# Splitting the first loads of an adaLN / windowed-attention / token-mixer kernel between two DMA queues, with a new instruction order

## The chip, the cores and the metric

The kernel runs on one core of a Trainium2 chip. The metric is the device time of one execution in microseconds. Times before: 201.69, 201.56 and 201.41 us, median 201.56.

A core has five instruction streams that run beside each other and meet through semaphores: TensorE (PE: matmuls, with weight loads as PEld), VectorE (DVE), ScalarE (ACT), GpSimd (POOL) and SyncE (SP). SyncE issues DMAs and nothing else; ScalarE can issue DMAs too, on a queue of its own that is part of its instruction stream.

## What is computed

```python
def reference(A_x, A_wqkv, A_wo, B_x, B_w1, B_b1, B_w2, B_b2, c, w_mod):
    mod = (silu(c) @ w_mod).reshape(1, 6, 1, 512)
    sa, ca, ga, sb, cb, gb = mod[:, 0], mod[:, 1], ..., mod[:, 5]
    h = layernorm(x) * (1 + ca) + sa
    x = x + ga * A(h, A_wqkv, A_wo)
    h = layernorm(x) * (1 + cb) + sb
    return x + gb * B(h, B_w1, B_b1, B_w2, B_b2)
```

`x` is 2048 tokens by 512 channels, bf16. `A` is attention with 32 heads of 16 channels, in which each token sees 8 earlier tokens at a distance of 0, 2, ..., 14. `B` normalises each token, then mixes over the tokens for each channel: 2048 to 1792 with a tanh GELU, and back to 2048.

## The kernel before

The tokens lie in 16 tiles of 128. Attention goes through them in five chunks of 2, 4, 4, 4 and 2 tiles (`SIZES`). For each chunk the kernel takes layer norm statistics per tile (`ln1s`, `ln1v`), the group's reciprocal deviation (`rstd1_`, two ScalarE activations) and its offset (`nb1_`, VectorE), normalises each tile (`n1_`), transposes (`tr` and `hT` through TensorE for chunks 0 and 1, `xt` by DMA for the others), projects to q, k and v (`qkv<chunk>_<t><j>`, t = 0 query, 1 key, 2 value), evicts (`ev`), multiplies q and k on VectorE (`qk`), sums by matmul (`red`), does the softmax (`max`, `sub`, `exp`, `esum`, `rcp`, `smB`), multiplies with v on VectorE (`pv`), sums (`pvacc`), evicts (`oev`) and multiplies with the output weights (`wo`). A residual sum and two more layer norms follow (`x1`, `ln2`, `n2`, `aff`, `ln3`, `h3`), then the token mixer in two passes (`mlp1`, `mlp2`) and the stores.

At the start the condition `c` is loaded (`ld_c`), put through a SiLU (`cps`, `silu_exp`, `silu_dve`) and multiplied with the modulation weights: `ld_wmod1` loads the columns of the scale `ca`, `modcols1` and `a1col` make the column of 1 + ca from them, with which the weights or the transposed tiles are scaled (`wsc`, `hT`); `ld_wmod0`, `modcols0` and `sab` do so for the shift `sa`, and `qvb` makes the projections' bias of it. `ld_x0` and `ld_x1` load one tile each (chunk 0), `ld_x_<chunk>_<tile>` two tiles (256 KB); `ld_wqkv0`, `ld_wqkv1`, `ld_wqkv2` load the query, key and value weights, 512 KB each, as are `ld_wmod1` and `ld_wmod0`.

Every piece of work is added to a graph with the engines that could do it (`add_any`). Which engine does it and in which order the streams are issued is written by hand in the string `ORDER` (lines 191 to 249): a name takes the first engine of its list, and a letter behind a colon picks another (`a` ScalarE, `d` VectorE, `p` GpSimd, `s` SyncE; `q` on a matmul issues it as four column quarters). `schedule` (line 86) walks the string; each engine gets its own pieces in that order and works through them strictly in it. `fill:n` puts n units of 128 columns of matmuls with the identity matrix on TensorE, whose results nobody reads.

`dma` (line 376) issues on SyncE's queue; `dma2` (line 381) can issue on SyncE's or ScalarE's. The program that is built from this gives every DMA one of eight semaphores in turn, and a DMA that takes a semaphore for a second time waits, on the queue that issues it, until the earlier one has landed.

In the order before, ScalarE's queue holds `ld_x_1_2` and `ld_c`, then the load of the activation table, then its activations. SyncE's holds `ld_x1`, `ld_x0`, `ld_x_1_4`, `ld_wmod1`, `ld_x_2_8`, `ld_wqkv0`, `ld_x_2_6`, `ld_wqkv1`, `ld_wmod0` and the later loads.

Instructions are recorded through a wrapper, so that nearly all of them carry line 142 in the profile; they are told apart by tiles: `xx` the tokens, `big` (`wmodA`) the modulation columns and later the products, `wst` the raw projection weights, `h` the normalised tiles, `psS` and `psL` accumulators.

Of the kernel before, what the change touches and what calls it, by code (L numbers as in the profile page):

```python
# [196 lines left out]
qkv0_00 qvb0 wsc0_0:p ev0_10:a ld_b2 ld_wo1 hT1_1:d qkv1_00 ln1s11:d ln1s10:d ln1s13:d qkv1_10:q ln1v11 ln1v10
qvb_cp0:a ev0_00:a ln1s12:a ev0_02:d qkv1_13 ld_wqkv2 qkv0_20 ln1v13 qk0_3 qk0_2 ev1_13:a qk0_0 qvb1 ln1v12 qkv0_22:q
ld_wrow0 red0_0 ev1_00:a qkv1_03:q ev1_10:a qk0_1 red0_1 red0_2 red0_3 mask qvb_cp1:a ev0_20:a ev0_22:a wsc1_2:p
halo_v1:a qk1_0 ev1_03:a wsc1_3:a qkv1_11:q ld_wmod2 wsc2_3:a modrow0 ld_b1 mrows0:a ev1_11:a ld_wrow2 qkv1_02 max0  # L200
wsc0_2:p ld_wo0 n1_7:p sub0 rstd1_3 qkv1_01 ld_wo2 exp0 qkv1_12:q wsc1_1:p esum0:q qk1_3 red1_0 ev1_01:a qk1_1
ev1_02:a biascols n1_6:p ld_wrow1 rcp0 smB0 ev1_12:a ld_x_4_14 ln1s14:a qkv1_22 qk1_2 a2_0_2:a xt6 ld_wrow3 modrow1
red1_1 a2_0_1:a n1_9:p wsc2_0:d ln1s15:a ln1v14 nb1_3 n1_11:a qkv1_23:q mrows1 qkv1_21 ev1_21:a red1_2 red1_3 xt8
ev1_23:a fill:1 n1_10:p qkv1_20 ev1_20:a ev1_22:a qkv2_13 qkv2_10 wsc0_1:p vd0_2 ev2_13:a ln1v15 vd0_1 max1 sub1
qkv2_00 exp1 a2_0_0:s a2_0_3:s pv0_1 vd0_0 pv0_0 st_row0 pv0_2 qkv2_03 esum1:q ld_wo3 pvacc0_0 vd0_3 halo_v2:p
biascols_cp:a pvacc0_1 pv0_3 pvacc0_2 pvacc0_3 ev2_10:a ev2_00:a qk2_0 n1_13:a n1_12:a ld_row0 woq_s rcp1 smB1
oev0_2:a qkv2_11 qkv2_02:q ev2_03:a qk2_3 qkv2_01:q red2_0 oev0_0:a wo0:q wsc2_1:a wsc2_2:a qkv2_12 ev2_11:a ev2_01:a
ev2_02:a ev2_12:a wo1 qkv2_21:q a2_1_1:a qkv2_22 x1_1:a ln2q1:a x1_0:a xt10 ln2q0:a qk2_1 qkv2_23 xt12 qk2_2 a2_1_0:s
halo_k3:a ln2m0 vd1_2 a2_1_2:s qkv3_12 a2_1_3:s pv1_2 rstd1_4 red2_1 nb1_4 vd1_0 st_row1 red2_2 red2_3 rstd2_0
ev2_22:a nb2_0 ev2_21:a qkv3_13:q ev3_13:a max2 vd1_3 pv1_0 n1_14:a vd1_1 pvacc1_2 n1_15:a qkv2_20:q ev2_20:a sub2  # L210
qkv3_22:q ev3_12:a pv1_1 qkv3_10 exp2 ev2_23:a halo_v3:a qkv3_20 n2_0:a oev1_2:a ev3_10:a esum2 rcp2 qkv3_00 ev3_22:a
qkv3_02:q ev3_00:a pv1_3 ev3_02:a pvacc1_0 ev3_20:a qkv3_01:q ev3_01:a qkv3_11:q xt14 ld_row1 n2_1:p vd2_3 pvacc1_1
smB2 aff0 qk3_0 vd2_1 fill:1 vd2_0 oev1_0:a oev1_1:a pvacc1_3 ev3_11:a qk3_1 qkv3_23:q oev1_3:a a2_2_2:s ln3s1:a
qkv3_03:q wo4 a2_2_1:s qk3_2 a2_2_0:s ev3_03:a ev3_23:a x1_4:a ln2q4:a wo2 x1_2:a a2_2_3:s red3_0 wo3:q x1_3:a ln2q3:a
qkv3_21:q ev3_21:a wo5 red3_1 pv2_3 x1_5:a vd2_2 qk3_3 qkv4_20:q red3_2 qkv4_22 red3_3 qkv4_12 fill:18 ln2q5:a
ld_w1_0_512 ln2q2:a ln2m2 pv2_0 pvacc2_0 vd3_0 ev4_20:a ln3s0:a ln3v0 ev4_12:a rstd2_2 ev4_22:a ln3v1 qkv4_02 oev2_0:a
ln2m4 rstd2_4 nb2_2 n2_2:a max3 sub3:q exp3 pvacc2_3 oev2_3:a qkv4_10:q pv2_2 vd3_2 esum3 nb2_4 pv2_1 vd3_1 n2_3:p
ld_w1_0_0 n2_5:a rcp3 smB3 pvacc2_2 fill:14 a2_3_0:s a2_3_1:s a2_3_3:s n2_4:a qkv4_00:q oev2_2:a rstd3_0 aff2 pvacc2_1
oev2_1:a wo6 wo9 wo7 aff4 nb3_0 ln3s2:d ev4_02:a ln3s3:a ln3v3 h3_1:p wo8 a2_3_2:s ev4_00:a ln3v2 ld_w2_0 ln3s4:d
rstd3_2 nb3_2 x1_9:a ln3s5:a h3_0:p mlp1_0_6_0:q x1_7:a ln3v4 x1_8:a h3_3:d mlp1_0_1_0 h3_2:d mlp1_0_6_2 mlp1_0_1_2  # L220
pv3_1 mlp1_0_5_0:q ln3v5 ev4_10:a ld_w1_0_896 x1_6:a mlp1_0_3_0:q mlp1_0_3_2:q ln2q7:a pvacc3_1 rstd3_4 mlp1_0_5_2:q
oev3_1:a mlp1_0_2_0:q pv3_0 mlp1_0_2_2:q nb3_4 h3_4:a mlp1_0_0_0:q mlp1_0_0_2 h3_5:a mlp1_0_0_4:q qk4_0 ln2q8:a
ln2q6:a park0_0:a ln2q9:a mlp1_0_6_4:q mlp1_0_2_4:q mlp1_0_1_4:q park0_1:a pv3_2 mlp1_0_5_4:q vd3_3 pvacc3_0 oev3_0:a
mlp1_0_3_4:q ld_w2_1 park0_2:a pv3_3 red4_0 ln2m6 pvacc3_2 oev3_2:a mlp1_0_4_0:q qk4_1 pvacc3_3 ld_w1_0_1152
mlp1_0_4_2:q mlp1_0_4_4:q rstd2_6 oev3_3:a wo12:q halo_v4:p vd4_2 vd4_3 nb2_6 n2_9:a qk4_2 n2_7:d qk4_3 wo10:qn red4_1
ld_w1_0_1408 n2_6:a vd4_1 n2_8:a aff6 red4_2 red4_3 max4 park0_3:a ln3s8:d ln3s6:d x1_12:a ln3v8 wo11 vd4_0 ln3s9:d
mlp1_0_7_0 ld_w2_3 park0_4:a ln3v6 mlp1_0_7_2 park0_5:a ln3v9 x1_11:a ln2q12:a mlp1_0_8_0 mlp1_0_8_2 park0_6:a wo13:n
ln3s7:a ln3v7 sub4 mlp1_0_10_0 mlp1_0_9_0 x1_13:d exp4 rstd3_6 nb3_6 esum4 mlp1_0_8_4 ln2q13:a ln2m12 mlp1_0_10_2
mlp1_0_10_4 mlp1_0_9_2 rcp4 mlp1_0_7_4 h3_8:d rstd2_12 mlp1_0_12_0 mlp1_0_12_2 mlp1_0_12_4 smB4 a2_4_1:a a2_4_0:s
mlp1_0_9_4 a2_4_2:s h3_9:d a2_4_3:a h3_7:d nb2_12 h3_6:p mlp1_0_7_6 ln2q11:a park0_7:a x1_10:d mlp1_0_8_6 ld_w1_0_1664  # L230
ln2q10:a park0_8:a n2_13:p mlp1_0_9_6 park0_9:a n2_12:d aff12 ln2m10 rstd2_10 mlp1_0_10_6 park0_10:a ln3s13:a pv4_2
nb2_10 ld_w1_1_0 pv4_1 mlp1_0_11_0 mlp1_0_11_2 mlp1_0_11_4 mlp1_0_12_6 pv4_0 mlp1_0_11_6 ld_w1_1_640 inj1_6:qn pv4_3
pvacc4_0 pvacc4_1 n2_11:a mlp1_0_13_0:q pvacc4_2 pvacc4_3 n2_10:a mlp1_0_13_2:q park0_11:a mlp1_0_13_4 oev4_0:a
oev4_2:a aff10 ln3s10:a wo14 inj1_3:n ln3s11:d ln3v11 x1_14 ln2s14 wo15 x1_15 mlp1_0_13_6 ln2v14 ln3s12:a ln3v10
ln2s15 rstd2_14 nb2_14 ln2v15 n2_14:d rstd3_10 aff14 rstd2_15 nb2_15 inj1_4:qn ln3v13 park0_12:a mlp1_1_3_6 park0_13:a
mlp1_1_6_6 inj1_1:n mlp1_1_1_6 n2_15:p mlp1_1_4_6 inj1_0:n mlp1_1_0_6 nb3_10 h3_10:a mlp1_1_4_10 mlp1_1_3_10 ln3s14:d
ld_w2_4 mlp1_1_0_10 ln3v14 ln3v12 rstd3_12 h3_11:a mlp1_1_6_10 inj1_5:n mlp1_1_5_6 mlp1_1_5_10 rstd3_14 mlp1_1_1_10
aff15 nb3_12 ln3s15:d ln3v15 h3_12:p nb3_14 park1_0:+ h3_13:p rstd3_15 nb3_15 inj1_2:n mlp1_1_2_6 ld_w1_1_896 h3_14:p
h3_15:a ld_w1_2_0 park1_1:+ mlp1_1_2_10 park1_2:+ mlp1_1_7_10 park1_3:+ park1_4:+ park1_5:+ mlp1_1_8_10 mlp1_1_10_10
park1_6:+ padd1_7 padd1_10 gelu10 padd1_8 mlp1_1_9_10 padd1_9 gelu9 mlp1_2_4_11 mlp1_2_4_14 mlp1_2_1_11 mlp1_2_1_14  # L240
padd2_1 padd2_4 gelu7 mlp1_2_0_11 mlp1_2_0_14 padd2_0 gelu0 mlp1_2_2_11 gelu4 gelu8 mlp1_2_2_14 ld_w1_1_1408
mlp1_2_3_11 mlp1_2_3_14 padd2_3 gelu3 ld_w1_2_640 mlp1_2_6_11 padd2_6 gelu6 padd2_2 gelu2 mlp1_2_5_11 mlp1_1_11_10
padd1_11 mlp1_2_5_14 padd2_5 gelu1 gelu11 mlp1_1_12_10 ld_w2_5 ld_w2_7 mlp1_1_13_10 gelu5 mlp2_0_0 padd1_12 gelu12
mlp2_0_0b ld_w2_2 ld_w2_9 ld_w2_13 ld_w2_11 padd1_13 gelu13 mlp2_0_0c mlp2_6_0 mlp2_4_0 gsc fin0_0 st_out0_0 fin4_0
st_out4_0 mlp2_8_0 fin8_0 mlp2_3_0 fin3_0 mlp2_2_0 fin2_0 st_out2_0 mlp2_1_0 fin1_0 mlp2_7_0 st_out3_0 fin6_0
st_out6_0 fin7_0 mlp2_10_0 fin10_0 st_out7_0 mlp2_11_0 mlp2_5_0 st_out1_0 fin5_0 st_out5_0 mlp2_14_0 fin11_0
# [829 lines left out]
```

## Time and profile before

| | |
|---|---|
| median of three runs | 201.56 us |
| the profiled execution | 202.11 us |
| its span, first to last instruction | 200.4 us |
| TensorE busy | 191.0 us |
| VectorE busy | 159.6 us |
| ScalarE busy | 128.6 us |
| GpSimd busy | 18.6 us |
| DMA | 35.95 MB, mean 179 GB/s |

Times in the profile are microseconds from the start of the span. A row of the timeline reads: start, duration, engine, line, operation, what it writes and reads, shape, count, and in brackets the idle time of the engine before it with what ended it. Neighbouring instructions of one kind are merged into one row. A DMA's row (`SPq`, `ACTq`) tells how long its issue took, not when the data landed. In the chain of waits a row is start, duration and what the time went to. In the table by stretch a row is the stretch, its length, the busy time of each engine with its count of instructions, the granted TensorE clock, the DMA share and GB/s.

### The profile page before, as it was taken

How to read it: one execution, taken by the hardware profiler on the slowest of the kernel's cores; microseconds unless marked ns; L12 is line 12 of the kernel's file. 1: busy time of each engine (PE TensorE's matmuls, PEld its weight loads, DVE VectorE, ACT ScalarE, POOL GpSimd, SP SyncE). 2: the span in 40 equal slices, each digit the busy share in tenths (PEclk: the TensorE clock that was granted, in tenths of full speed). 3: DMA queues.
4: the chain of work that ended last, by engine and by line, in shares of the span. 5: the costliest groups of instructions: out<-in, count | busy, mean ns of one | idle time of the engine just before them, and what ended most of it. 6: DMA issues, size and time to landing. Idle time of an engine off the chain costs nothing.

```text
span 200.4 us, 4572 instructions
## 1 busy us (share of the span) xinstructions
PE 191.0 (95%) x1818; PEld 95.8 (48%) x1836; DVE 159.6 (80%) x241; ACT 128.6 (64%) x306; POOL 18.6 (9%) x45
## 2 busy tenths in 40 slices
...
GB/s 161 341 355 350 176 240 127 160 56 185 300 143 321 220 167 194 176 112 311 64 310 257 36 184 196 160 186 234 338 244 298 85 26 52 27 52 52 174 52 52
DMA packets 53889, 35.95 MB, mean 179 GB/s; under 512 B 24428, under 2 KB 50668, under 8 KB 53868
## 3 DMA queue, kind: packets, MB, share of 16 engines
...
q8 instruction: 14, 0.23, 0.5%
...
## 4 chain that ended last, share of the span: by engine, by line
PE 69%; DVE 22%; issue 4%; DMA 1%; ACT 1%; ACTq 0%; DVEq 0%
PE psS L142 67%; DVE big L142 14%; PE psL L142 3%; DVE st L142 2%; DVE h L142 2%; DMA c_t<-in_c_dram 1%; DVE mv L142 1%; ACT h L142 1%; DVE lsb L142 1%; DVE m L142 1%; DVE nb L142 0%; ACTq L142 0%; DVE woq L142 0%; DVE hT L142 0%; ACT rb L142 0%
## 5 line engine op out<-in xcount | busy, mean ns | idle before, releaser
L142 PEld LDWEIGHTS <-wst 128*128 128x128 bf16 (+1 forms) x536 | 34.9, 101 | 33.7 <-issue 4.0
L142 PE MATMUL psS<-h,wst 128*128 128x512 bf16 (+1 forms) x333 | 50.3, 380 | 0.5 <-issue 0.3
L142 DVE TENSOR_TENSOR big<-q_sb,k_f 128x4096 bf16<-128x4096 bf16 (+1 forms) x20 | 36.6, 1859 | 0.4 <-ACT q_sb L142 0.4
L142 DVE TENSOR_TENSOR big<-a2sb,vD 128x4096 bf16<-128x4096 bf16 (+1 forms) x20 | 36.5, 1860 | 0.2
L142 PE MATMUL psS<-hT,w_qkv 128*32 128x512 bf16 (+3 forms) x360 | 29.7, 346 | 0.0
L142 DVE SCALAR_TENSOR_TENSOR h<-psS,bcol,rows_bc 128x512 f32<-128x512 f32 (+2 forms) x17 | 12.1, 710 | 22.1 <-PE psS L142 20.6
L142 PEld LDWEIGHTS <-w_qkv 128*32 128x32 bf16 (+1 forms) x402 | 19.4, 109 | 17.8 <-issue 4.4
L142 PE MATMUL psS<-gT,big 128*128 128x512 bf16 x110 | 24.7, 379 | 0.1
L142 PEld LDWEIGHTS <-big 128*128 128x128 bf16 x144 | 12.0, 97 | 13.5
L142 ACT ACTIVATE junk<-xx 128x512 bf16<-128x512 bf16 x26 | 16.3, 627 | 3.3 <-DVE xx L142 1.4
L142 PE MATMUL psS<-woq,o_sb 128*32 128x512 bf16 (+1 forms) x107 | 15.7, 380 | 0.9 <-ACT o_sb L142 0.6
L142 ACT ACTIVATE gT<-psS,bcol 128x512 bf16<-128x512 f32 x14 | 9.0, 685 | 8.1 <-DVE psS L142 8.0
L142 POOL TENSOR_SCALAR h<-xx,rs,nb 128x512 bf16<-128x512 bf16 x9 | 6.9, 766 | 75.6 <-DVE nb L142 36.5
L142 DVE TENSOR_TENSOR psS<-psS,gT 128x512 f32<-128x512 f32 x14 | 9.3, 695 | 5.0 <-PE psS L142 5.0
L142 ACT ACTIVATE h<-xx,nb,rs 128x512 bf16<-128x512 bf16 x16 | 12.4, 808 | 0.5 <-DVE nb L142 0.4
L142 PEld LDWEIGHTS <-ident 128*32 128x32 bf16 (+1 forms) x137 | 7.0, 102 | 10.5 <-issue 5.9
L142 PE MATMUL psS<-ident 128*128 128x512 bf16 (+1 forms) x35 | 10.6, 450 | 1.4 <-POOL epscol L142 1.4
L142 PE MATMUL psS<-hT,wst 128*32 128x512 bf16 (+2 forms) x110 | 11.7, 352 | 0.1
L142 DVE TENSOR_TENSOR h<-h,xx 128x512 bf16<-128x512 f32 (+2 forms) x17 | 11.1, 653 | 0.6
L142 DVE TENSOR_TENSOR h<-h,rows_bc 128x1024 bf16<-128x1024 bf16 (+2 forms) x16 | 10.9, 689 | 0.4
L142 DVE BATCH_NORM_STATS2 st<-xx 128x6 f32<-128x512 bf16 x12 | 7.9, 680 | 3.9 <-DMA xx<-in_A_x_dram 3.8
L142 ACT ACTIVATE v_sb<-psS,qvb 128x512 bf16<-128x512 f32 (+1 forms) x20 | 11.0, 595 | 0.0
...
## 6 DMA issues: line engine op xcount, KB each, us to landing
...
xx<-in_A_x_dram SPq DMA_DIRECT2D x6, 256.0 KB, 7.9
...
```

Source lines behind the costliest of these rows:

```text
L142: r = fn(*a, **k)
```

## The change

`dma2` takes the graph's keyword arguments, and `ld_c`, `ld_wmod` and `ld_wqkv` are built with it, so that either queue can issue them:

```diff
-    def dma2(out_ap, in_ap, nbytes, writes, name):
+    def dma2(out_ap, in_ap, nbytes, writes, name, **kw):
         return G.add_any([(n_, 0.5, lambda q_=q_: q_.dma_start(out_ap, in_ap)) for n_, q_ in QS], writes=writes, name=name,
-                         bytes_=nbytes / 350e3, lat=2.0, desc=1 + nbytes // 16384)
+                         bytes_=nbytes / 350e3, lat=2.0, desc=1 + nbytes // 16384, **kw)
...
-    add("act", 0.55, lambda: nc.scalar.dma_start(c_t[:], c[0].rearrange("(t p) -> t p", p=P)), writes=["c_t"],
-        name="ld_c", lat=2.0)
+    dma2(c_t[:], c[0].rearrange("(t p) -> t p", p=P), D * 4, ["c_t"], "ld_c")
...
-        dma(wmodA[:, :, v * D:(v + 1) * D], wmod_view[:, :, v * D:(v + 1) * D], D * D * 2, [], [("wmodA", v)],
+        dma2(wmodA[:, :, v * D:(v + 1) * D], wmod_view[:, :, v * D:(v + 1) * D], D * D * 2, [("wmodA", v)],
             f"ld_wmod{v}", **(dict(behind=first) if first else dict(alloc=s_wm)))
...
-        dma(wraw[t], wqkv_view[:, :, t * D:(t + 1) * D], D * D * 2, [], wkey[t], f"ld_wqkv{t}")
+        dma2(wraw[t], wqkv_view[:, :, t * D:(t + 1) * D], D * D * 2, wkey[t], f"ld_wqkv{t}")
```

The whole of `ORDER` is new. Its first lines:

```diff
-ident ld_x_1_2:a halo0 ld_c consts ld_x1:s ld_x0:s ld_x_1_4:s act_table ln1s3:d fill:4 cps ld_wmod1 silu_exp silu_dve
-fill:64 ln1s1:a ln1s2:a ln1s0:d ln1v1 ld_x_2_8 ln1v0 ln1s4:d ld_wqkv0 rstd1_0 nb1_0 n1_1:a fill:4 ln1v4 n1_0:p ln1s5:d
-ln1v2 ln1v5 ln1v3 rstd1_1 nb1_1 ld_x_2_6 modcols1 n1_2:d n1_5:d ln1s8:a a1col wsc0_3:p n1_4:d tr0_0 hT0_1:a hT0_3:a
-n1_3:d hT0_0:a fill:13 hT0_2:a ld_wqkv1 ld_wmod0 ln1s9:d ld_x_3_10 ln1s6:d tr1_0 tr1_2 hT1_2:a ln1v6 qkv0_02 ln1v9
+act_table ld_c:a ident ld_x1:s ld_x_1_2:a ld_wmod1:a cps silu_exp ld_x_1_4:s silu_dve ln1s3:d ld_x0:s ln1s1:d ln1s0:d
+ln1s2:a fill:16 ld_wqkv0:a ln1v3 ln1v1 fill:14 ln1v0 ln1v2 ld_b2 consts ln1s4:d rstd1_0 nb1_0 ld_x_2_8 ln1s5:d fill:23
+n1_1:a ln1v4 ln1v5 n1_0:p rstd1_1 nb1_1 ld_wqkv1:s n1_3:a ln1s8:d modcols1 a1col n1_5:p ln1v8 n1_2:a tr0_0 hT0_3:d
+wsc1_1:a n1_4:p fill:16 ld_x_2_6 hT0_2:d tr1_0 hT1_0:a tr1_2 hT1_3:a hT0_1:d hT0_0:d qkv0_10 qkv0_12 ln1s6:d hT1_1:a
...
```

By queue, the changed program's first entries are these. ScalarE: the table load, `ld_c`, `ld_x_1_2`, `ld_wmod1`, `silu_exp`, `ln1s2`, `ld_wqkv0` (it waits for the semaphore of `ld_x_2_8`), `rstd1_0`, `n1_1`, `rstd1_1`, `n1_3`, `n1_2`. SyncE: `ld_x1`, `ld_x_1_4`, `ld_x0`, `ld_b2`, `ld_x_2_8`, `ld_wqkv1`, `ld_x_2_6`, `ld_wmod0`, then the later loads. VectorE starts with `silu_dve`, `ln1s3`, `ln1s1`, `ln1s0`, where it started with `ln1s3`, `silu_dve`, `ln1s0`. The first projections of chunk 0 are those of the keys (`qkv0_10`, `qkv0_12`), where they were a query's (`qkv0_02`).

Fillers ahead of `modcols1` are 53 units (16 + 14 + 23) in place of 4 before the condition and 68 behind it; between `tr0_0` and `tr1_0` 16 in place of 13; behind the first projections 9 (4 + 5) in place of 34 (1 + 1 + 18 + 14). 46 pieces change their engine, among them 13 from ScalarE to VectorE and 10 the other way, 6 from ScalarE to GpSimd and 5 back. 58 matmul groups are issued in column quarters in place of 49. The computation is the same.

107 lines of the change are left out of this document (54 added, 53 removed).

## The prediction

> **What bounds the kernel now.** I read the page first, then busy time by stretch, then the first rows of the chain of waits, then the timeline of the first 19 us.
>
> ```profile
> span 200.4 us, 4572 instructions
> ...
> PE 191.0 (95%) x1818; PEld 95.8 (48%) x1836; DVE 159.6 (80%) x241; ACT 128.6 (64%) x306; POOL 18.6 (9%) x45
> ```
>
> The busy table by stretch (start:end, length, then busy us of PE, PEld, DVE, ACT, POOL):
>
> ```profile
> 18.80:40.00 21.20, 20.92 (x336) 11.48 (x335) 20.80 (x22) 18.75 (x45) 2.00 (x3) 1.00 0.78 188
> 40.00:60.00 20.00, 19.43 (x265) 9.39 (x259) 19.76 (x16) 18.41 (x40) 0.77 (x1) 1.00 0.56 169
> 60.00:80.00 20.00, 19.69 (x271) 10.20 (x274) 19.83 (x19) 19.40 (x50) 0.77 (x1) 1.00 0.65 226
> 80.00:100.00 20.00, 19.23 (x280) 9.56 (x272) 19.91 (x25) 19.44 (x52) 1.70 (x3) 1.00 0.64 168
> 100.00:122.00 22.00, 21.45 (x194) 10.10 (x194) 21.38 (x43) 19.41 (x50) 1.53 (x2) 1.00 0.75 207
> 134.00:197.00 63.00, 62.74 (x314) 29.93 (x318) 34.57 (x52) 9.00 (x14) 0.00 (x0) 1.00 0.49 140
> ```
>
> From 18.8 to 122 us VectorE idles 0.40 + 0.24 + 0.17 + 0.09 + 0.62 = 1.5 us in 103; TensorE 2.5. From 134 on TensorE alone is full (0.3 us idle). So the kernel is a head, then 103 us that VectorE fills, then 75 us of TensorE. Work is only permuted behind the head, so the end moves with the moment at which VectorE starts its first product, `qk0` (18.80), less what a better order takes from 1.5 us.
>
> What sets that moment:
>
> ```profile
> 1.33 2.60 DMA c_t<-in_c_dram
> ...
> 3.98 7.09 PE psS L142 x34
> ```
>
> ```profile
> 7.15 0.28 ACT L142 ACTIVATE lv<-mv,epscol 128x2 f32<-128x2 f32 x1
> 7.46 0.20 ACT L142 ACTIVATE rs<-lv 128x2 f32<-128x2 f32 x1
> ...
> 7.70 0.16 DVE L142 SCALAR_TENSOR_TENSOR nb<-mv,rs 128x2 f32<-128x2 f32 x1 [1.00 <-ACT rs L142]
> ...
> 7.87 0.66 DVE L142 BATCH_NORM_STATS2 st<-xx 128x6 f32<-128x512 bf16 x1
> 7.90 0.81 ACT L142 ACTIVATE h<-xx,nb,rs 128x512 bf16<-128x512 bf16 x1 [0.23 <-DVE nb L142]
> ...
> 8.66 0.23 DVE L142 BATCH_NORM_AGGREGATE mv<-st 128x2 f32<-128x6 f32 x2
> 8.93 0.30 ACT L142 ACTIVATE lv<-mv,epscol 128x4 f32<-128x4 f32 x1 [0.22 <-DVE mv L142]
> ...
> 9.50 0.16 DVE L142 SCALAR_TENSOR_TENSOR nb<-mv,rs 128x4 f32<-128x4 f32 x1 [0.60 <-ACT rs L142]
> ```
>
> ```profile
> 12.07 1.28 PE L142 MATMUL psS<-ident,h 128*128 128x128 bf16 x16
> ...
> 13.19 2.78 PE L142 MATMUL psS<-hT,wst 128*128 128x256 bf16 x24
> ...
> 18.80 3.50 DVE L142 TENSOR_TENSOR big<-q_sb,k_f 128x2048 bf16<-128x2048 bf16 x3
> ```
>
> The condition lands at 3.93; fillers then hold TensorE until `modcols1`. Beside it runs the layer norm of tiles 0 to 5: `rstd1_0` (7.15), `nb1_0` (ends 7.86), the second group's `rstd1_1`, `nb1_1` (ends 9.66), the norms, the transposes (12.07), the first projection (13.19), and 5.61 us later `qk0`. Those 5.61 us (three projections, `modcols0`, `qkv0_00`, `qvb0`, the q eviction) hold the same operations after the change, so the question is when the first projection starts.
>
> **The change, part by part.**
>
> *Condition first.* It is issued behind a 256 KB pair now and ahead of it afterwards, but behind the table load (1.28 us). Whether that load holds the queue no row shows; the nearest is a DMA that ScalarE's queue issues during an activation:
>
> ```profile
> 31.12 0.63 ACT L142 ACTIVATE junk<-xx 128x512 bf16<-128x512 bf16 x1
> 31.59 0.74 ACTq L142 DMA_DIRECT2D a2sb<-lsb  x1
> 31.66 0.19 ACT L142 ACTIVATION_READ_ACCUMULATOR junk<-xx 128x1 f32 x1
> 32.37 0.82 ACTq L142 DMA_DIRECT2D a2sb<-lsb  x1
> 33.24 0.63 ACT L142 ACTIVATE junk<-xx 128x512 bf16<-128x512 bf16 x1 [1.39 <-issue]
> ```
>
> Issue at about 0.85 (not held) gives a landing by 0.85 + 2.60 = 3.45; held, 1.28 later, 4.7. I take not held. Either way the gain of 0.5 or loss of 0.8 us meets VectorE's next wait: `silu_dve` now stands ahead of all statistics there, and the last of the first three, `ln1s0`, waits for tile 0, which has moved behind the pair 4 and 5.
>
> *The query weights go to ScalarE's queue* (the change's words say key weights; the order gives `ld_wqkv0`, the query third, to ScalarE, `ld_wqkv1`, the keys, to SyncE; both land long before their use, so the words change nothing in time). This is the step that I think decides. The same rows show why: behind a DMA that waits on ScalarE's queue (31.59, released by VectorE) nothing starts until it is issued, 1.39 us idle. And the moved load has to wait. The built program gives loads eight semaphores in turn; the ninth user of a semaphore waits until the earlier load on it has landed. Now these waits stand on SyncE, where only loads queue behind them:
>
> ```profile
> 4.33 1.10 SPq L142 DMA_DIRECT2D wst<-in_A_wqkv_dram  x1
> ...
> 12.49 0.37 SPq L142 DMA_DIRECT2D wst<-in_w_mod_dram  x1
> ```
>
> ```profile
> wst<-in_A_wqkv_dram SPq DMA_DIRECT2D x1, 512.0 KB, 8.1
> ```
>
> ```profile
> SPq L142 <- DMA wst<-in_A_wqkv_dram: 0.2, 1, 0.2
> ```
>
> 4.33 + 8.1 = 12.4: the load at 12.49 was let go by that landing. In the changed program `ld_wqkv0` shares its semaphore with `ld_x_2_8`, and so waits on ScalarE for tiles 8 and 9. Queued behind it there are `rstd1_0`, `n1_1`, `rstd1_1`, `n1_3`, `n1_2`: the whole norm chain, and through it VectorE's `nb1_0`, GpSimd's `n1_0`, TensorE's transposes.
>
> When do tiles 8 and 9 land? Ahead of or with them on SyncE: 128 + 256 + 128 + 4 + 256 = 772 KB; on ScalarE's queue beside them up to 1 + 256 + 512 = 769 KB. Scale for bytes: the query weights landed at 3.26 + 7.1 = 10.4 with 2048 KB in, the keys at 12.4 with 2816, so 768 KB in 2.0 us.
>
> ```profile
> 3.26 0.47 SPq L142 DMA_DIRECT2D wst<-in_A_wqkv_dram  x1
> ```
>
> ```profile
> wst<-in_A_wqkv_dram SPq DMA_DIRECT2D x1, 512.0 KB, 7.1
> ```
>
> All 1541 KB in: 10.4 - 507/384 = 9.1. With the 512 KB scale still to come: 1029 KB, 7.7. ScalarE's pair was served at once beside SyncE's loads, 3.0 us from issue to landing, so that queue isn't starved and the upper end is nearer:
>
> ```profile
> xx<-in_A_x_dram ACTq DMA_DIRECT2D x1, 256.0 KB, 3.0
> ```
>
> I take 8.7. Issuing 512 KB took 0.47 (3.26) to 1.10 (4.33); ScalarE's ring is nearly empty, so 0.47. `rstd1_0` then starts at 8.7 + 0.05 + 0.47 = 9.2 (from 7.7 + 0.5 = 8.2 to 9.1 + 1.15 = 10.25) in place of 7.15. Tile 0 alone, with at most 1024 KB in by 7.7 and then one statistic (0.66) and the aggregates (0.3), would hold it until 8.7 or so, so undoing the wait alone would not give all of it back.
>
> The Trainium skill, page "DMA: Bandwidth & Descriptors", section "Issuing engines are not separate DMA queues", says that loads started from several engines share the same DMA engines and save issue time alone. By it the bytes keep their pace, tiles 8 and 9 land at the upper of my two ends and the sum is +1.4 - 0.3, or 202.7; no run here yet shows two rings full for long.
>
> *The norm chain is shortened.* From `rstd1_0`'s start to `nb1_0`'s end 0.71 (7.15 to 7.86). Then `ln1s5`, two aggregates: to 8.75 against 8.93 now, as two small operations have moved ahead; with 0.73 to `nb1_1`'s end that is 1.62. Tiles 2 to 5 go to ScalarE and GpSimd, two each: 0.81 + 0.74 = 1.55 (+ 0.03). Transposes to first projection 13.19 - 12.07 = 1.12. Sum 4.32 from `nb1_0`'s end; now 13.19 - 7.86 = 5.33. So the reshuffle is worth 1.0 us. VectorE meanwhile does `ln1s8`, `a1col` and four `hT0` evictions, some 2.2 us against 2.7 available: hidden, and if it were late the first projection would wait for it.
>
> First projection: 9.2 + 0.71 + 4.32 = 14.2, against 13.19: **+1.0** (from 8.2: 13.2, 0.0; from 10.25: 15.3, +2.1).
>
> *Inner fillers fall from 34 units to 9.*
>
> ```profile
> 75.31 2.29 DVE L142 TENSOR_TENSOR big<-a2sb,vD 128x4096 bf16<-128x4096 bf16 x1
> ...
> 76.61 1.14 PE L142 MATMUL psS<-ident 128*128 128x512 bf16 x6
> ...
> 77.68 0.62 PE L142 MATMUL psS<-big,group 128*32 128x512 bf16 x8
> ```
>
> The largest fills a wait: the product that the next accumulation reads ends at 75.31 + 2.29 = 77.60, the accumulation starts at 77.68. Taken out, TensorE stands there instead: 0 (at most its 1.1 us).
>
> *Order searched anew, engines swapped.* Counted from `qk0` to `aff10`, VectorE has the same operations but two of 0.4 us exchanged. It can win at most the 1.5 us of idle, or lose as much where new order meets new waits; I take -0.3. Nine more matmul groups are issued in four column quarters, which costs weight loads that lie beside matmuls: 0.
>
> **Sum.** +1.0 - 0.3 = +0.7. The profiled execution took 202.11 for its 200.4 of span, so it would become 202.8; the median of the runs is 201.56, so 202.3.
>
> **The rivals.**
>
> *Faster.* The two queues bring tiles 0, 8 and 9 by about 6.5, the wait on ScalarE is over before its work, `rstd1_0` stays at 7.15, and the shortened chain comes through: 7.86 + 4.32 = 12.2, -1.0, with -0.3: 200.3. For it: ScalarE's pair at 3.0 us. Against it: bytes.
>
> *Even.* The wait ends at the lower bound: 0.0 and -0.3 to +0.3, 201.5. For it: rates once two rings are full are not shown. Against: nothing shows the scale yielding.
>
> *Slower by another cause: a slow TensorE.* Fillers ahead of `modcols1` fall from 68 units to 53. Now a filler step takes 0.43 us until 9.62 (8.77 to 9.19, 9.19 to 9.62); from then on three weight loads stand in 0.57 us:
>
> ```profile
> 8.77 0.15 PEld L142 LDWEIGHTS <-ident 128*128 128x128 bf16 x1 [0.28 <-issue]
> ...
> 9.19 0.15 PEld L142 LDWEIGHTS <-ident 128*128 128x128 bf16 x1 [0.28 <-issue]
> 9.62 0.57 PEld L142 LDWEIGHTS <-ident 128*128 128x128 bf16 x3 [0.28 <-issue]
> ```
>
> ```profile
> 144.85 10.74 PE psS L142 x49
> ```
>
> A matmul of the same size takes 10.74 / 49 = 0.22 later. The step up came 5.6 us after 3.98; 53 units last 5.7 us at the slow pace. If they run out before it, the projections begin at half pace, and 5.6 us of work at half pace lose up to 2.8: 205.1. The granted clock in the rows reads 1.00 throughout and doesn't show the step. The Trainium skill, "TensorE: Matmul & The Clock Gate", "What's actually happening", has the array at half rate until one free-running window of some 3.4 us is busy; by it the step comes 3.4 to 6.8 us after the start of steady work, and 5.7 us may miss it. The trace agrees with its 5.6.
>
> **How the numbers follow.** Forecast 0.50 (own range 201.9 to 203.6, from its bounds less 0.3 and up to the same added), faster 0.15, even 0.22, slow TensorE 0.13. About 0.2% (0.4 us) is what a measurement tells from no change. Faster: 0.15 + 0.03 of the even case = 0.18; within: 0.19 + 0.02 = 0.21; slower: 0.61. Range 200.6 to 204.3: it leaves out about half of the faster case below and most of the slow TensorE above, 0.17.
>
> **What would show it.** ScalarE idle ahead of `rstd1_0` behind its second 512 KB load, with that row's issue late (near 9); `rstd1_0` 2 us later than now; first projection near 14.2 and `qk0` near 19.8; VectorE as full as now behind it. I am wrong if `rstd1_0` starts before 8, if the first projection starts before 13, if VectorE's idle between `qk0` and `aff10` differs by over 1 us, or if filler steps of 0.43 us are followed by projections at that pace.

## The result, and the profile after

The changed kernel takes 203.66 us (median of four runs, 202.79 to 204.29), the kernel before 201.49 beside it: ratio 1.0104, 95% interval 1.0063 to 1.0146. The profiled execution took 203.33 us against 202.11. The forecast was 202.3, and 202.8 for the profiled execution.

The page of the changed kernel, its span and busy times:

```profile
span 201.6 us, 4733 instructions
...
PE 190.0 (94%) x1906; PEld 95.4 (47%) x1906; DVE 159.5 (79%) x245; ACT 126.6 (63%) x299; POOL 18.9 (9%) x45
```

No engine that was busy for long works longer than before (GpSimd alone, by 0.3 us); the 1.2 us are waiting. The busy table by stretch, in the prediction's columns, counted from the new start of `qk0`:

```profile
20.04:40.00 19.96, 19.96 (x377) 11.11 (x370) 19.87 (x21) 17.77 (x40) 0.77 (x1) 1.00 0.66 185
40.00:60.00 20.00, 19.93 (x250) 9.73 (x249) 19.90 (x17) 18.73 (x44) 1.62 (x3) 1.00 0.63 172
60.00:80.00 20.00, 18.61 (x243) 10.01 (x242) 19.62 (x18) 19.46 (x51) 1.38 (x2) 1.00 0.92 264
80.00:100.00 20.00, 18.87 (x263) 8.64 (x266) 19.91 (x26) 18.80 (x50) 1.71 (x3) 1.00 0.65 172
100.00:122.70 22.70, 22.70 (x271) 11.02 (x267) 22.11 (x43) 20.27 (x52) 0.77 (x1) 1.00 0.55 157
```

VectorE is as full as before: idle 0.09 + 0.10 + 0.38 + 0.09 + 0.59 = 1.25 us, where it was 1.5. So the loss is the head. Its timeline:

```profile
0.81 1.28 ACT L142 ACT_TABLE_LOAD   x1 [0.81 <-PEq L1060]
0.84 0.57 ACTq L142 DMA_DIRECT2D c_t<-in_c_dram  x1
...
5.66 1.88 DVE L142 BATCH_NORM_STATS2 st<-xx 128x6 f32<-128x512 bf16 x3 [2.15 <-DMA xx<-in_A_x_dram]
...
8.07 0.37 ACTq L142 DMA_DIRECT2D wst<-in_A_wqkv_dram  x1
8.14 0.60 PE L142 MATMUL psS<-sc,big 128*128 128x1 bf16 x16
8.56 0.30 ACT L142 ACTIVATE lv<-mv,epscol 128x2 f32<-128x2 f32 x1 [1.43 <-DVE st L142]
...
10.21 0.62 PE L142 MATMUL psS<-ident,h 128*128 128x128 bf16 x8 [1.47 <-POOL h L142]
...
12.48 1.07 PE L142 MATMUL psS<-ident,h 128*128 128x128 bf16 x16 [0.78 <-ACT h L142]
...
13.38 1.91 PE L142 MATMUL psS<-hT,wst 128*128 128x256 bf16 x16
...
16.09 1.06 PE L142 MATMUL psS<-hT,wst 128*128 128x256 bf16 x8 [0.80 <-DMA wst<-in_A_wqkv_dram]
```

Three things are to be seen. `rstd1_0` (8.56) stands behind the issue of the query weights on ScalarE's queue (8.07), as predicted. The condition was issued at 0.84, during the table load, so that load does not hold the queue. And at 16.09 TensorE waits for something the prediction had waved through: the query weights themselves. The chain of waits (start, duration, what it was) names both, from the issue of tiles 8 and 9 on:

```profile
2.71 5.35 DMA xx<-in_A_x_dram
8.07 7.97 DMA wst<-in_A_wqkv_dram
16.09 7.23 PE psS L142 x132
```

The first projection starts 0.19 us later than before (13.38 against 13.19), and `qk0` at 20.04 in place of 18.80, 1.24 later. The span grew by 1.2.

Behind `qk0` half a microsecond is gained and mostly given back at the end. The last rows of TensorE and VectorE, before and after:

```profile
196.38 0.94 PE L142 MATMUL psS<-woq,wst 128*128 128x128 bf16 x14
...
197.36 0.29 DVE L142 TENSOR_TENSOR h<-psS,fpre 128x128 bf16<-128x128 f32 x1
```

```profile
197.12 0.94 PE L142 MATMUL psS<-woq,wst 128*128 128x128 bf16 x14
197.50 0.43 DVE L142 TENSOR_TENSOR h<-h,xx 128x256 bf16<-128x256 f32 x1 [0.42 <-DMA out_dram<-h]
...
198.48 0.28 DVE L142 TENSOR_TENSOR h<-psS,fpre 128x128 bf16<-128x128 f32 x1
```

TensorE ends 0.74 later (of 1.24), VectorE 1.11 later, since one of its last sums now waits 0.42 us for a store.

### The profile page after: what moved, and what is told of

Same layout as the page of the kernel before. It is cut to its first block, busy times and chain, and to the rows that moved or that the text cites. A ratio compares the mean times of both kernels' runs of the same rounds, so it can differ in the third digit from the quotient of the medians.

```text
span 201.6 us, 4733 instructions
## 1 busy us (share of the span) xinstructions
PE 190.0 (94%) x1906; PEld 95.4 (47%) x1906; DVE 159.5 (79%) x245; ACT 126.6 (63%) x299; POOL 18.9 (9%) x45
## 4 chain that ended last, share of the span: by engine, by line
PE 51%; DVE 21%; DMA 13%; ACT 6%; issue 4%; SPq 3%; DVEq 0%
PE psS L142 50%; DVE big L142 16%; DMA wst<-in_A_wqkv_dram 4%; SPq L142 3%; DMA xx<-in_A_x_dram 3%; DMA vD<-v_sb 2%; DMA a2sb<-lsb 2%; ACT h L142 2%; DVE h L142 2%; DMA out_dram<-h 2%; DVE m L142 1%; ACT q_sb L142 1%; DVE lsb L142 1%; ACT k_f L142 1%; PE psL L142 1%
## 5 line engine op out<-in xcount | busy, mean ns | idle before, releaser
L142 ACT ACTIVATE junk<-xx 128x512 bf16<-128x512 bf16 x24 | 15.1, 629 | 4.0 <-DMA xx<-in_A_x_dram 2.9
L142 PE MATMUL psS<-woq,o_sb 128*32 128x512 bf16 (+1 forms) x160 | 16.6, 380 | 0.0
L142 ACT ACTIVATE h<-xx,nb,rs 128x512 bf16<-128x512 bf16 x20 | 15.4, 809 | 1.2 <-DVE nb L142 0.9
L142 ACT ACTIVATE v_sb<-psS,qvb 128x512 bf16<-128x512 f32 (+1 forms) x20 | 11.5, 597 | 1.2 <-PE psS L142 1.2
L142 ACT ACTIVATE q_sb<-psS,qvb 128x512 bf16<-128x512 f32 (+1 forms) x18 | 10.6, 610 | 2.0 <-PE psS L142 1.2
L142 PEld LDWEIGHTS <-group 128*32 128x32 bf16 x288 | 6.9, 96 | 8.8 <-issue 3.2
L142 PE MATMUL psS<-big,group 128*32 128x512 bf16 (+1 forms) x160 | 9.6, 338 | 0.9 <-DVE big L142 0.9
```

The costliest lines, as they stand in the source:

```text
L142: r = fn(*a, **k)
```

## The experiments

All kernels were timed in five rounds against the kernel before, whose medians in these sets were 201.49, 201.62, 201.87 and 201.61 us; the ratios are to the set's own. The head of each profiled execution (us; the starts are those of its timeline; "end" is the span, the time of the last instruction's end):

| kernel | `rstd1_0` | first projection | `qk0` | end | end - `qk0` | median of runs | ratio to before, interval |
|---|---|---|---|---|---|---|---|
| before | 7.15 | 13.19 | 18.80 | 200.4 | 181.6 | 201.49 | |
| changed | 8.56 | 13.38 | 20.04 | 201.6 | 181.6 | 203.66 | 1.0104, 1.0063 to 1.0146 |
| changed again | 8.31 | 13.13 | 20.07 | 201.5 | 181.4 | 203.52 | 1.0122, 1.0095 to 1.0148 |
| query weights on SyncE | 7.50 | 12.32 | 18.00 | 199.7 | 181.7 | 201.54 | 0.9994, 0.9975 to 1.0012 |
| 68 units ahead of `modcols1` | 8.56 | 13.39 | 19.78 | 201.1 | 181.3 | 203.54 | 1.0109, 1.0080 to 1.0138 |
| query weights late on ScalarE | 7.58 | 13.10 | 26.65 | 209.2 | 182.5 | 210.31 | 1.0441, 1.0421 to 1.0460 |
| gaps filled | 8.11 | 12.94 | 19.79 | 200.9 | 181.2 | 202.68 | 1.0059, 1.0036 to 1.0082 |
| SyncE, tile 0 second, one gap filled | 8.06 | 12.89 | 18.54 | 200.2 | 181.6 | 201.74 | 1.0019, 0.9992 to 1.0047 |
| before, query weights on ScalarE | 9.63 | 17.74 | 25.64 | 207.2 | 181.6 | 210.04 | 1.0390, 1.0356 to 1.0423 |
| before, fewer fillers | 7.28 | 12.57 | 18.18 | 199.8 | 181.6 | 201.43 | 0.9985, 0.9972 to 0.9999 |
| SyncE, pair first | 7.12 | 12.75 | 18.42 | 200.7 | 182.3 | 202.48 | 1.0034, 1.0003 to 1.0066 |
| head mended | 6.83 | 12.74 | 18.41 | 199.5 | 181.1 | 201.62 | 0.9992, 0.9976 to 1.0009 |
| query weights early on ScalarE | 7.57 | 12.39 | 18.06 | 200.0 | 181.9 | 202.38 | 1.0032, 1.0007 to 1.0057 |
| head mended, second | 6.78 | 12.25 | 17.95 | 199.5 | 181.6 | 201.07 | 0.9973, 0.9958 to 0.9988 |

The sixth column checks the prediction's premise, that the end moves with `qk0`: over a shift of 8.7 us it stays within 181.1 and 182.5, so nearly everything else is read from the head. The four sets did not all run on the same chip, so kernels of different sets are compared by their ratios.

### The changed kernel again

> The changed kernel itself, for its spread. Theory A (the loss is the head: the query weights land at 16.04 and the projection of the queries waits for them, qk0 starts at 20.04 in place of 18.80): its profiled execution again has qk0 near 20.0 and the runs lie near 203.3. Theory B (a part of the median's 2.2 us comes from executions in which TensorE is at full pace a step later, because 53 filler units run out early): the runs fall into groups, those with a mean granted clock of about 0.991 some 0.7 to 1.5 us above those with 1.000.

The head is the same (`qk0` at 20.07). The runs, with the first kernel's, lie by mean granted clock: 203.33, 203.17 and 203.44 at 1.000; 202.79 and 203.53 at 0.996 to 0.997; 203.51, 203.98, 204.29, 204.68 and 204.77 at 0.983 to 0.992. The last five average 204.25, the others 203.25. All runs of the kernel before have 0.998 or more. So the median lies above the profiled execution: in half of the executions TensorE was granted less, and these are 1.0 us slower on average. 0.992 is what one stretch of 3.41 us at half clock would make (3.41 x 0.5 / 203 = 0.008); such a stretch is seen in the run with the weights late, below. A mean of 0.996 to 0.999 needs no such stretch: in the four profiled executions that have one, the clock is 1.00 until 198 us and falls only behind it, where TensorE has nothing left to do.

### The query weights on SyncE's queue

```diff
-ln1s2:a fill:16 ld_wqkv0:a ln1v3 ln1v1
+ln1s2:a fill:16 ld_wqkv0:s ln1v3 ln1v1
```

> The changed kernel with the query weights on SyncE's queue at the same place of the order (there they are issued ahead of tiles 8 and 9 and wait for nothing). Theory A: rstd1_0 no longer stands behind an issue and starts when tile 0's statistics are there, 7.9 to 8.1 (8.56 in the changed kernel); first projection 12.7 to 12.9 (13.38); no wait for query weights (0.96 us gone); qk0 at 18.3 to 18.6 (20.04); the profiled execution 1.4 to 1.7 us shorter than the changed kernel's 203.3. Theory B: the spread stays, and the median is still 0.7 us or more above the time that qk0's start gives. Rival (the query weights are late because the loads as a whole are more than the first 16 us can bring): they land near 16 again and the time stays within 0.4 us of the changed kernel.

Three rows of its timeline:

```profile
7.50 0.30 ACT L142 ACTIVATE lv<-mv,epscol 128x2 f32<-128x2 f32 x1 [0.72 <-DVE mv L142]
...
12.32 2.78 PE L142 MATMUL psS<-hT,wst 128*128 128x256 bf16 x24
...
18.00 6.83 DVE L142 TENSOR_TENSOR big<-q_sb,k_f 128x2048 bf16<-128x2048 bf16 x5
```

`rstd1_0` is 1.06 earlier, and the projections of queries and keys are one row of 24 without a wait: `qk0` is 2.04 earlier, 1.06 of it ahead of the first projection and 0.98 from the late weights. All three starts are earlier than expected. Of the 1.06, the block makes at least 0.70: the first statistics, too, started 0.36 earlier in this execution (5.30 against 5.66), and that start varies from one execution to the next (5.18 to 5.66 in six with the pair in the same place). The profiled execution takes 201.52, the median is that of before: with this one load moved back, the whole loss is gone. The rival, that the weights land as late wherever they are issued, is refuted.

### More fillers ahead of the scale's columns

```diff
-... rstd1_0 nb1_0 ld_x_2_8 ln1s5:d fill:23
+... rstd1_0 nb1_0 ld_x_2_8 ln1s5:d fill:38
```

> The changed kernel with 38 filler units in place of 23 ahead of modcols1, so 68 in all as before the change. Theory A: nothing moves in the head but the fillers' end (8.35 to about 9.2, and modcols1 with it, which nobody waits for before 10.9); time within 0.4 us of the changed kernel. Theory B: executions with a mean granted clock below 0.999 become rare, the median falls by 0.5 to 1.0 us and the spread shrinks to about 0.4 us, that of the kernel before.

The median is 203.54: no gain. In the profiled execution the fillers came to full pace early, and TensorE stood 2.3 us ahead of `tr0`, at a clock of 1.00. None of the six runs has a clock below 0.995, where five of the changed kernel's ten have 0.983 to 0.992; six runs don't settle whether the fillers did that. Yet the three slowest (203.82, 204.24 and 204.94) have 1.000, 0.995 and 0.997. So there are slow executions that no stretch at half clock explains, and their cause was not found.

### The query weights later on ScalarE's queue

```diff
-ln1s2:a fill:16 ld_wqkv0:a ln1v3 ... ln1v8 n1_2:a tr0_0
+ln1s2:a fill:16 ln1v3 ... ln1v8 n1_2:a ld_wqkv0:a tr0_0
```

> The changed kernel with the query weights' load moved behind n1_2 on ScalarE's queue, so that the norm chain does not stand behind it but the load is issued 2 to 4 us later (near 11). Theory A by lateness (what costs is when the weights land): first projection 12.7 to 13.0, but the weights land at 16.5 to 19.5, qk0 at 20.5 to 23.5, time 0.5 to 3.5 us above the changed kernel. Theory A by the block, as predicted (what costs is the norm chain standing behind the issue): rstd1_0 near 8.0, qk0 at 18.3 to 19.5, time 0.5 to 1.7 us below the changed kernel.

The block is gone (`rstd1_0` 7.58) and the kernel is 6.8 us slower than the changed one beside it (203.52): the landing is what costs. The load was issued at 11.79, and the projection waited 6.00 us; `tr0` had waited 1.58:

```profile
9.23 0.74 PE L142 MATMUL psS<-ident,h 128*128 128x128 bf16 x8 [1.58 <-POOL h L142]
...
11.79 0.38 ACTq L142 DMA_DIRECT2D wst<-in_A_wqkv_dram  x1
...
21.01 1.90 PE L142 MATMUL psS<-hT,wst 128*128 128x256 bf16 x8 [6.00 <-DMA wst<-in_A_wqkv_dram]
```

That is 9.2 us after its issue, 1.5 later than the latest landing expected. `qk0` is 6.6 us later than in the changed kernel: 4.9 of it is the later landing (21.01 against 16.09), the other 1.7 the clock. In the busy table the granted clock stands behind the counts of the five engines (0.50 or 1.00):

```profile
9.59:13.00 3.41, 3.41 (x24) 2.13 (x22) 3.27 (x12) 2.35 (x5) 3.01 (x6) 0.50 1.08 346
13.00:19.83 6.83, 2.01 (x20) 1.75 (x18) 1.34 (x5) 3.92 (x10) 0.02 (x1) 1.00 1.08 348
19.83:26.66 6.83, 5.65 (x52) 3.80 (x52) 2.97 (x11) 2.10 (x4) 3.68 (x5) 0.50 0.46 139
```

Behind the wait TensorE ran at half pace until 26.66: the projection at 21.01 takes 1.90 in place of 1.06. Here the fall of the clock behind waits of TensorE is seen directly.

### The gaps filled

```diff
-... ln1v8 n1_2:a tr0_0 hT0_3:d wsc1_1:a n1_4:p fill:16 ... rstd1_2 qkv0_02
+... ln1v8 n1_2:a fill:24 tr0_0 hT0_3:d wsc1_1:a n1_4:p fill:28 ... rstd1_2 fill:14 qkv0_02
```

> The changed kernel with filler units in the three idle stretches of TensorE in its head: 24 units ahead of tr0 (idle 1.47 to 2.3 us there), 28 in place of 16 between tr0 and tr1 (0.78 us), 14 ahead of the query projection (0.8 to 1.1 us). Theory B, now with another cause (an idle TensorE in the head lets the granted clock fall to one half for a stretch in some executions, mean clock 0.983 to 0.997, 0.2 to 1.3 us longer): all executions at a mean clock of 0.998 or more, median 203.1 to 203.4, spread at most 0.5 us. Rival (the spread comes from elsewhere, as 15 more units ahead of modcols1 did not shrink it): median 203.4 to 203.7 and clocks as low as 0.992 again. If the fillers themselves are late (half pace), the first projection is up to 1 us later in some executions.

Nine of ten runs have a clock of 1.000, one 0.997, where half of the changed kernel's had 0.992 or less: with these gaps filled, the stretches at half clock are gone. The median is 202.68, and its interval (up to 1.0082) lies below that of the changed kernel run again (from 1.0095). That gain is not the clock's alone, though. Six of the nine runs at 1.000 lie at 202.41 to 202.69, below the changed kernel's 203.17 to 203.44 at the same clock; in the profiled executions `qk0` is 0.25 earlier, as the query's projection is (15.84 against 16.09), and the stretch behind `qk0` is 0.4 shorter, which was not traced. The spread did not shrink as expected: three runs at 1.000 lie at 203.35 to 204.20, and what they wait for no profile shows.

### SyncE's queue, tile 0 second, one gap filled

```diff
-act_table ld_c:a ident ld_x1:s ld_x_1_2:a ... ld_x_1_4:s silu_dve ln1s3:d ld_x0:s ... ld_wqkv0:a ... fill:16
+act_table ld_c:a ident ld_x1:s ld_x0:s ld_x_1_2:a ... ld_x_1_4:s silu_dve ln1s3:d ... ld_wqkv0:s ... fill:28
```

> The changed kernel with the query weights on SyncE's queue, tile 0 second there again, and 28 filler units between tr0 and tr1. Theory A: rstd1_0 at 6.9 to 7.3 (7.50 with the query weights on SyncE's queue alone), first projection 11.8 to 12.1 (12.32), qk0 17.5 to 17.8 (18.00), profiled execution 201.0 to 201.3; with theory B the spread shrinks as well and the median is 200.8 to 201.2, faster than the kernel before. Rival (tile 0's place costs nothing, since the chain then waits for tiles 2 to 5 or for TensorE): qk0 at 18.0, median 201.3 to 201.6.

This was a miss. The first statistics (`ln1s3`, of the pair 2 and 3) started at 5.87, later than with tile 0 third (5.18 to 5.66 in six profiled executions), and `rstd1_0` with them. Moving tile 0 up gained nothing; the pair on ScalarE's queue is what the statistics wait for. Four of twelve runs have clocks of 0.990 to 0.992, so with this gap filled the clock still falls in some executions.

### The kernel before with that one load moved

```diff
-ln1s4:d ld_wqkv0 rstd1_0 nb1_0
+ln1s4:d ld_wqkv0:a rstd1_0 nb1_0
```

> The kernel before with nothing changed but the query weights' load on ScalarE's queue, at its old place of the order. There it shares its semaphore with tiles 6 and 7, which land near 9.7. Theory A: ScalarE stands until about 9.7, rstd1_0 at about 10.2 (7.15); the weights, issued at 9.7 behind some 1.5 MB of SyncE's loads, land at 16 to 18; the first projection, here the query's, starts at 16 to 18 (13.19) and qk0 at 21.6 to 23.6 (18.80); the time is 204.3 to 206.5. Rival (another part of the change did it, and this load alone costs little): within 0.5 us of the kernel before.

```profile
9.13 0.40 ACTq L142 DMA_DIRECT2D wst<-in_A_wqkv_dram  x1
9.63 0.30 ACT L142 ACTIVATE lv<-mv,epscol 128x2 f32<-128x2 f32 x1 [2.36 <-DMA xx<-in_A_x_dram]
...
17.74 5.08 PE L142 MATMUL psS<-hT,wst 128*128 128x256 bf16 x24 [3.02 <-DMA wst<-in_A_wqkv_dram]
...
25.64 2.36 DVE L142 TENSOR_TENSOR big<-q_sb,k_f 128x2048 bf16<-128x2048 bf16 x2
```

```profile
wst<-in_A_wqkv_dram ACTq DMA_DIRECT2D x1, 512.0 KB, 8.6
```

```profile
15.61:22.44 6.83, 4.70 (x23) 3.37 (x24) 3.26 (x11) 2.12 (x5) 4.59 (x7) 0.50 0.89 295
```

Besides this letter the run has the change's `dma2` for the load, without which it could not be issued on ScalarE's queue. Block, landing and first projection came about as worked out (9.63, 9.13 + 8.6 = 17.7, 17.74). `qk0` and the time are above what was expected (21.6 to 23.6 and 204.3 to 206.5), as TensorE's 3.02 us wait took the clock as well: the 24 products need 5.08 us in place of 2.78. The profiled execution took 208.95, which is 202.11 and the 6.84 us by which `qk0` is later; why the median, 210.04, lies 1.1 above it was not traced. One letter in the order costs the old kernel 8.4 us.

### The kernel before with fewer fillers

```diff
-fill:64 ln1s1:a ... n1_3:d hT0_0:a fill:13 hT0_2:a
+fill:44 ln1s1:a ... n1_3:d hT0_0:a fill:18 hT0_2:a
```

> The kernel before with 48 filler units ahead of modcols1 in place of 68, and 18 in place of 13 behind tr0. Theory C (in the profiled execution of before the fillers ran at 0.43 us a step until 9.68 and held modcols1 until 10.52; VectorE's a1col waited for it, and n1_4 and n1_3 stood behind a1col, so the fillers set the first projection, by 0.74 us; in executions in which the full pace comes earlier they don't, and these make the lower times): modcols1 at 9.0 to 9.4, first projection 12.4 to 12.7, qk0 18.0 to 18.3, the profiled execution 201.3 to 201.6 like the other runs, median 201.2 to 201.5, and no run near 202.1. Rival (the two groups of times have another cause): profiled execution 202.0 to 202.2 again.

The rows of `modcols1` and `a1col` before, and those of this run with the first projection:

```profile
10.52 0.54 PE L142 MATMUL psS<-sc,big 128*128 128x1 bf16 x16
...
11.10 0.16 DVE L142 TENSOR_SCALAR a1col<-psS 128x4 f32<-128x4 f32 x1 [0.66 <-PE psS L142]
```

```profile
9.31 0.60 PE L142 MATMUL psS<-sc,big 128*128 128x1 bf16 x16
...
10.48 0.15 DVE L142 TENSOR_SCALAR a1col<-psS 128x4 f32<-128x4 f32 x1
...
12.57 2.78 PE L142 MATMUL psS<-hT,wst 128*128 128x256 bf16 x24
```

All twelve runs lie at 201.28 to 201.51, the profiled one at 201.51 (`qk0` 18.18, not 18.80); the 27 runs of before beside them spread from 201.07 to 202.40. So in the profiled execution of before the fillers themselves held `modcols1` until 10.52 and cost 0.6 us. That other executions of before paid this in part or not at all is inferred from their times; there is one profile of before. The prediction took that execution's head for every execution's.

### The pair first, and the head mended

Three edits on the kernel with SyncE's queue: the pair ahead of the condition; then tile 0 second and more filler units as well; then `ln1s8` behind `a1col` and the query projected first.

```diff
-act_table ld_c:a ident ld_x1:s ld_x_1_2:a ld_wmod1:a cps silu_exp ld_x_1_4:s silu_dve ln1s3:d ld_x0:s
+act_table ld_x_1_2:a ld_c:a ident ld_x1:s ld_wmod1:a fill:16 cps silu_exp ld_x_1_4:s ln1s3:d silu_dve ld_x0:s
```

```diff
-... ld_wmod1:a fill:16 cps ... fill:23 ... n1_2:a tr0_0 ... fill:16 ... tr1_0
+... ld_x0:s ld_wmod1:a fill:20 cps ... fill:30 ... n1_2:a fill:8 tr0_0 ... fill:28 ... tr1_0
```

```diff
-n1_3:a ln1s8:d modcols1 a1col ... fill:28 ... hT0_0:d qkv0_10 qkv0_12
+n1_3:a modcols1 a1col ... fill:18 ... hT0_0:d ln1s8:d ln1v8 qkv0_02 qkv0_10 qkv0_12
```

> The changed kernel with the query weights on SyncE's queue and, beside that, the pair 2 and 3 issued ahead of the condition on ScalarE's queue as before the change (its statistics ahead of silu_dve on VectorE, 16 of the 53 filler units ahead of cps). Theory D (putting the condition first made the pair land near 5.3 in place of 3.8 and so moved the first statistics by 1.5 to 1.8 us): ln1s3 starts at 3.7 to 4.2 (5.30 with the condition first), rstd1_0 at 6.7 to 7.2 (7.50), first projection 11.5 to 12.2 (12.32), qk0 17.2 to 17.8 (18.00), profiled execution 200.7 to 201.3 (201.52). Rival (tile 0, which lands as late as before, or the condition's chain sets rstd1_0): rstd1_0 stays at 7.4 to 7.6 and the time at 201.3 to 201.6.

> As the run with the pair first, with tile 0 second on SyncE's queue and more filler units: 20 ahead of cps, 44 behind it, 8 between modcols1 and tr0, 28 between tr0 and tr1, so that TensorE never stands for more than 0.3 us from 1.5 us on. Theories A, B and D together: qk0 at 17.2 to 17.8, profiled execution 200.7 to 201.3, mean clock 0.998 or more in nearly all executions, median 200.7 to 201.2 and a spread of at most 0.6 us: faster than the kernel before by 0.2 to 0.4%. Rival (executions at a lower clock have another cause than the head's gaps): a third of the runs lie 1 to 2 us above the rest with clocks near 0.991.

> As the mended head before, whose a1col stood on VectorE behind ln1s8, which waited for tile 8 until 10.70 (a1col at 11.31), and whose keys landed at 12.12. Now ln1s8 stands behind the four hT0, the query is projected first, and 18 filler units stand between tr0 and tr1 in place of 28. Theories A, B and D: a1col at 9.3 to 9.6, tr1 at 10.9 to 11.2, first projection 11.8 to 12.2 (12.74), qk0 17.3 to 17.8 (18.41), profiled execution 200.3 to 200.9, mean clock 0.998 or more, median 200.5 to 201.1, 0.3 to 0.6% under the kernel before. Rival (the next wait, the keys or the transposed tiles of chunk 1, takes it back): qk0 at 18.2 or later and a median within 0.2% of the kernel before.

The timeline of the first of the three:

```profile
3.81 0.69 DVE L142 BATCH_NORM_STATS2 st<-xx 128x6 f32<-128x512 bf16 x1 [3.81 <-DMA xx<-in_A_x_dram]
...
7.12 0.30 ACT L142 ACTIVATE lv<-mv,epscol 128x2 f32<-128x2 f32 x1 [0.98 <-DVE mv L142]
...
10.71 0.69 DVE L142 BATCH_NORM_STATS2 st<-xx 128x6 f32<-128x512 bf16 x1 [1.28 <-DMA xx<-in_A_x_dram]
...
11.32 0.14 DVE L142 TENSOR_SCALAR a1col<-psS 128x4 f32<-128x4 f32 x1
```

The pair's statistics do start 1.5 us earlier (3.81 against 5.30), so putting the condition first did cost that much. But the gain ran into the next wait: `ln1s8` on VectorE, waiting for tile 8 until 10.71, with `a1col` queued behind it. The first projection was 0.4 us later than before that edit, not earlier, and the times were a miss. The second kernel has the same wait; its twelve runs, though, all have a clock of 0.998 or more and lie within 0.8 us. The third takes that wait out (`a1col` 9.68): `qk0` 17.95, median 201.07, ratio 0.9973 (0.9958 to 0.9988), less gained than expected, but faster than the kernel before by 0.3%. On TensorE `tr1` (11.36) stood behind the fillers, and the first projection, expected at 11.8 to 12.2, came at 12.25.

### The query weights early on ScalarE's queue

```diff
-ld_x_1_2:a ld_wmod1:a cps ... fill:16 ld_wqkv0:a ln1v3
+ld_x_1_2:a ld_wmod1:a ld_wqkv0:a cps ... fill:16 ln1v3
```

> The changed kernel with the query weights still on ScalarE's queue, but issued right behind the scale. There they wait for the pair 4 and 5 (near 5.3), and silu_exp stands behind them. Theory A by lateness: the weights, issued at 5.3, land near 9 to 11, so the query projection waits for nothing; the block falls on silu_exp (2.6 to about 5.8) and through silu_dve on the statistics, which wait until 5.3 to 5.7 for their tiles anyway: rstd1_0 at 8.0 to 8.7, first projection 12.8 to 13.5, qk0 18.5 to 19.2, profiled execution 202.0 to 202.7, between the changed kernel (203.3) and the one with SyncE's queue (201.5). Rival (a load on ScalarE's queue is served late wherever it is issued): it lands after 14 again and the time stays within 0.4 us of the changed kernel.

```profile
4.26 0.38 ACTq L142 DMA_DIRECT2D wst<-in_A_wqkv_dram  x1
...
12.39 2.78 PE L142 MATMUL psS<-hT,wst 128*128 128x256 bf16 x24
```

```profile
wst<-in_A_wqkv_dram ACTq DMA_DIRECT2D x1, 512.0 KB, 9.3
```

Issued at 4.26, the weights landed at 13.5, later than the 9 to 11 expected, and still in time for the query projection. `rstd1_0` (7.57), the first projection (12.39) and `qk0` (18.06) are those of SyncE's queue. So what costs is not the queue as such but the moment of issue; why the load took 9.3 us here, longer than when issued later, was not traced. The median is 202.38 all the same, with seven of twelve clocks at 0.990 to 0.992. In the profiled execution TensorE's gaps ahead of `tr0` and `tr1` (0.75 and 0.78 us) are still there; but with SyncE's queue they were 0.60 and 0.78, and only two of twelve runs had such a clock, so the gaps of one profile don't tell how often the clock falls.

## Why the prediction was right, and where it was not

**The bound.** This was right. The end moves with `qk0`; 181.6 us lie between them before and after.

**Query weights on ScalarE's queue.** Right in mechanism, and this load alone is the loss. The block was a little shorter than taken: tiles 8 and 9 let the load go at 8.07 (taken 8.7), `rstd1_0` came at 8.56 (taken 9.2), both within the bounds. Its aside, that tile 0 would hold `rstd1_0` until 8.7 without the wait, was too late by a microsecond: without the wait it came at 7.50 and 7.58.

**"Both land long before their use".** This is the step that failed, for the query weights; the projections of the keys, at 13.38, wait for no load. The prediction asked when the load is let go and what stands behind it, and not when its bytes arrive. They arrive 8.0 us after the issue:

```profile
wst<-in_A_wqkv_dram ACTq DMA_DIRECT2D x1, 512.0 KB, 8.0
```

The prediction's own rows had 7.1 and 8.1 us for such loads on SyncE's queue. Issued at its 8.7, the weights would land at 15.8 to 16.8, and the query's projection, third now, was due at 14.2 + 2/3 x 2.78 = 16.05: a wait of up to 0.75, from rows that it showed. The Trainium skill, "DMA: Bandwidth & Descriptors", "Issuing engines are not separate DMA queues", says that DMAs of all issuing engines share the same DMA engines and interleave; the 8.0, 8.6 and 9.3 us measured on ScalarE's queue, about as long as SyncE's 7.1 and 8.1, agree.

**Condition first.** Taken as meeting the next wait anyway, which hid what it did: the pair behind it landed 1.5 us later, and the statistics with it. In the changed kernel the block covered this, for the three statistics ended at 7.54 (5.66 + 1.88) and the block only at 8.44 (8.07 + 0.37).

**The norm chain.** From `rstd1_0` to the first projection 4.82 us, worked out as 0.71 + 4.32 = 5.03. Of the 1.0 us that the reshuffle was to win, half was no property of the old order: where the fillers end early the old chain takes 12.57 - 7.28 = 5.29, not 6.04, so the reshuffle is worth 0.5 by this estimate.

**First projection** +0.2 in place of +1.0, **from there to `qk0`** +1.05 in place of 0, **order** 0 in place of -0.3 (0.5 gained, most of it lost again in the last stores' wait). The sum is +1.2 in place of +0.7 for the profiled execution. So that the forecast came out on the right side is in part luck: of the 1.0 us that it expected at the first projection, 0.2 came, and most of the 1.2 is the wait for the query weights that it had put at nothing.

**From there to the median** the prediction went 0.55 us down, as the kernel before does. That failed too: before, the profiled execution was a slow one, by the reading above for a reason that the change removed (fillers ahead of `modcols1`), and after the change the median is 0.3 above the profiled one, as half of the executions had a lower clock. Of the 1.4 us between 202.3 and 203.66, 0.5 lie in the profiled execution and 0.9 in this step.

**Its own range.** The mechanism's range, 201.9 to 203.6, is narrower than its bounds: 0.0 less 0.3 to 2.1 plus 0.3, around 201.56, make 201.3 to 204.0. The measured 203.66 lies just outside the first and inside the second.

**The rivals.** Faster and even: the wait was not over early. Slow TensorE: a price of its kind, 1.0 us on average, was paid in half of the executions. Its cause, fillers that run out too early, is not what the lower clocks show: the granted clock reads 1.00 also while the first fillers run at the slow pace, so a late step up would not lower the mean. Fifteen more units ahead of `modcols1` left the median where it was; filling the gaps further on brought every clock to 0.997 or more. The Trainium skill, "TensorE: Matmul & The Clock Gate", "What's actually happening", has the clock fall after an idle window of some 3.4 us. The runs agree on the length of the stretches at half clock (3.41 and 6.83 us) but show one behind an idle time of 1.58 us alone: in the run with the weights late on ScalarE's queue `tr0` waited from 7.65 to 9.23, and the clock was 0.50 from 9.59.

**What stays open.** In unprofiled executions only the mean clock is known, not where it fell. Which idle stretch makes it fall, and in which executions, is open too: TensorE stood for 2.3 us in a profiled execution without a fall. Three runs with the gaps filled and three with 68 units are up to 2.1 us slower than the fastest of their kernel without a stretch at half clock that would explain it, and with the pair first the runs at 0.996 or more spread from 201.01 to 203.77; no profile shows why. The second and the third mended kernel have the same span (199.5) though `qk0` lies 0.46 us apart; where the third loses it was not traced.
